# One addition and one reciprocal for both groups of heads of a tile, in the first batch of a pooled attention with a feed-forward network

## The chip, the cores and the metric

The kernel runs on one core of one Trainium2 chip. The metric is the device time of one execution in microseconds (us). The engines are TensorE (PE, with PEld for its weight loads), VectorE (DVE), ScalarE (ACT), GpSimd (POOL) and SyncE (SP, which here issues nearly all DMAs).

## What is computed

Attention over pooled keys and values, and then a feed-forward network on its output, all in float32. There are 8 batches of 8 heads with 576 queries of 64 numbers; keys and values are averaged over 8 neighbours, so each query sees 72 keys.

```python
k_p = k.reshape(B, H, Sp, pool, D).mean(axis=3)          # Sp = 72
v_p = v.reshape(B, H, Sp, pool, D).mean(axis=3)
scores = scale * np.matmul(q, k_p.transpose(0, 1, 3, 2))
scores = scores - np.max(scores, axis=-1, keepdims=True)
attn = np.exp(scores)
attn = attn / (np.sum(attn, axis=-1, keepdims=True) + 1e-09)
...
x = attn_out.transpose(0, 2, 1, 3).reshape(B * S, H * D)  # 4608 x 512
h = x @ w_in                                              # 512 x 2048
g = np.maximum(0.01 * h, h)
return g @ w_out                                          # 2048 x 512
```

## The kernel before

**The whole.** The network's two products take nearly all of TensorE's time. Each factor is split into a high and a low part and a product is three matmuls (lines 905 to 907 for the first layer, 931 to 933 for the second). The weights are split on the chip too: `convert` (lines 201 to 212) turns a raw block of `w_in` or `w_out` into its two parts with two ACT steps, three DVE steps, one more ACT step (line 211) and one more DVE step (line 212). The intermediate `w_t` lies in PSUM in this part of the program.

**The first batch.** Nothing of the network can start before the first 512 rows of `x` are there, so batch 0 is done by itself ahead of it, from 0 to about 46 us, while the first blocks of weights are converted beside it (`c` in the list below). Its 576 queries are five tiles `t` of 128 rows (the last has 64), in three pieces `j`: tiles 0 and 1, tiles 2 and 3, tile 4. A tile's eight heads are two groups `g` of four. The steps are:

- `q{t}`: transposes the queries of a tile on TensorE (`pq`, line 514) and copies them to `qT`.
- `sa{t}{g}` (`s_unit`): the scores of one group on TensorE (`pss`, line 542), minus the row maximum by DVE (line 550), the exponentials by ACT, one instruction a head, with the row sums read out after each (line 552). Maximum and sum lie in a tile `red`.
- `sb{t}{g}` (`norm_unit`): DVE adds 1e-9 to the four sums (line 563) and takes their reciprocals (line 564), POOL multiplies the exponentials with them into `at`, in two instructions (lines 566 and 570).
- `pu{t}{g}`: transposes `at` on TensorE (`pp`, line 634) and splits it into a high part by ACT (636) and a low part by DVE (639 and 643).
- `au{j}{g}`: multiplies with the pooled values (`pa`, lines 658 to 661) and splits the result into `xh` (ACT, 675) and `xl` (DVE, 676).
- `vu`: places the pooled values: `pvm` on TensorE (448), `v_hi` by ACT (456), `v_lo` by DVE (459), `v_parts` (480, 481), `pv` (486) and `v_rem` (489).

**What sets the order.** The list FIRST writes the steps out. TensorE executes in exactly the order of the list (its schedule is manual). For ACT, DVE, POOL and SP a scheduler with a cost model of its own chooses the order from the dependencies and the place in the list; each engine then works strictly in that order, so an instruction that waits holds up all that stand behind it on its engine. The PSUM tiles of batch 0 go round six banks (`bank`): a TensorE step can start when the step six before it has been read out. So `pp` of tile 1, group 1, takes the bank of `pvm`, which `v_lo` is the last to read; `pss` of tile 4 takes the banks of the last two `pa`, which `xl` reads last.

Batch 1 uses `norm_unit` as well, group by group, and later batches `norm_via`; both take the 1e-9 from the tile `tiny`.

Of the kernel before, what the change touches and what calls it, by code (L numbers as in the profile page):

```python
# [10 lines left out]
F32 = mybir.dt.float32  # L11
# [4 lines left out]
ALU = mybir.AluOpType  # L16
# [8 lines left out]
def tile_pooled_attention_ffn(  # L25
# [9 lines left out]
    nc = tc.nc  # L35

    P = 128
# [24 lines left out]
        WHOLE, WHOLE, WHOLE,  # L62
    ]
    FIRST = (
# [3 lines left out]
    )  # L68
# [6 lines left out]
    const = ctx.enter_context(tc.tile_pool(name="const", bufs=1))  # L75
    wts = ctx.enter_context(tc.tile_pool(name="wts", bufs=1))
    one = ctx.enter_context(tc.tile_pool(name="one", bufs=1))
    two = ctx.enter_context(tc.tile_pool(name="two", bufs=2))
# [3 lines left out]
    four = ctx.enter_context(tc.tile_pool(name="four", bufs=4))  # L82
# [6 lines left out]
    make_identity(nc, ident)  # L89


    marks = const.tile([P, 5], F32, name="marks")
    copies = marks[:, 0:4]
    nc.vector.tensor_reduce(
        out=copies, in_=ident.rearrange("p (h c j) -> p c h j", h=4, c=4), axis=AX.XY, op=ALU.add
# [42 lines left out]
        "lo": const.tile([P, 2, PMAX], F32R, name="pT_lo"),  # L138
    }

    tiny = const.tile([P, 4], F32, name="tiny")
    nc.gpsimd.memset(tiny, 1e-9)

    warm = const.tile([P, 1], F32, name="warm")
# [79 lines left out]
    def bank(b, name):  # L224
        nonlocal turn
        pool, tag = banks[turn % len(banks)] if b == 0 else banks[0]
        turn += 1
        return pool.tile([P, NK, P], F32, tag=tag, name=name)
# [271 lines left out]
    def q_unit(b, t, qr):  # L500
# [17 lines left out]
        else:  # L518
# [3 lines left out]

    WIDE = {("at", 1): (8, 0), ("at", 2): (8, 1), ("at", 3): (7, 0),
            ("e", 1): (7, 1), ("e", 2): (6, 0), ("e", 3): (6, 1)}
    wides = {}

    def wide_at(b, t, nm):
        return b == 0 and (nm, t) in WIDE

    def wide(b, t, g, nm, shape):  # L530
        if (nm, t) not in wides:
            wides[nm, t] = spare(*WIDE[nm, t], [P, 2, *shape], F32, f"{nm}{b}_{t}")
        return wides[nm, t][:, g]

    def s_unit(b, t, g, qT):

        n = tiles[b][t][1]
        pss = bank(b, f"pss{b}_{t}_{g}")
        sc = pss.rearrange("a p x -> a (p x)")[:, : 4 * SP]
        for i in range(2):  # L540
            p = 2 * g + i
            nc.tensor.matmul(  # L542
                sc[:, 2 * SP * i : 2 * SP * (i + 1)], qT[:, p, :],
                kT[:, p, :, :].rearrange("d i s -> d (i s)"), start=True, stop=True,
            )
        scv = sc.rearrange("a (h s) -> a h s", s=SP)
        e = wide(b, t, g, "e", [4, SP]) if wide_at(b, t, "e") else two.tile([P, 4, SP], F32, tag="e", name=f"e{b}_{t}_{g}")
        red = four.tile([P, 2, 4], F32, tag="red", name=f"red{b}_{t}_{g}")
        mx, sm = red[:, 0, :], red[:, 1, :]
        nc.vector.tensor_reduce(out=mx[:n], in_=scv[:n], axis=AX.X, op=ALU.max, negate=True)  # L550
        for h in range(4):
            ins = nc.scalar.activation(  # L552
                e[:n, h, :], scv[:n, h, :], AF.Exp, bias=mx[:n, h : h + 1],
                accum_out=sm[:n, h : h + 1],
            )
        if b == 0:
            anchor["act"] = ins
        return e, sm

    def norm_unit(b, t, g, e, sm):  # L560
        n = tiles[b][t][1]
        eng = nc.vector if b == 0 and t in NORM_DVE else nc.gpsimd
        nc.vector.tensor_tensor(sm[:n], sm[:n], tiny[:n], op=ALU.add)
        nc.vector.reciprocal(sm[:n], sm[:n])
        at = wide(b, t, g, "at", [3, P]) if wide_at(b, t, "at") else three.tile([P, 3, P], F32, tag="at", name=f"at{b}_{t}_{g}")
        eng.tensor_tensor(
            at[:n, 0:2, :].rearrange("a i (h s) -> a (i h) s", h=2), e[:n, :, 0:MAIN],
            sm[:n].unsqueeze(2).broadcast_to([n, 4, MAIN]), op=ALU.mult,
        )
        ins = eng.tensor_tensor(  # L570
            at[:n, 2, :].rearrange("a (h c s) -> a h c s", h=4, c=4),
            e[:n, :, MAIN:].unsqueeze(2).broadcast_to([n, 4, 4, REM]),
            sm[:n].unsqueeze(2).unsqueeze(3).broadcast_to([n, 4, 4, REM]), op=ALU.mult,
        )
        if b == 0:
            anchor[eng] = ins
        return at

    def norm_via(b, t, g, e, sm):

        n = tiles[b][t][1]
        nc.vector.tensor_tensor(sm[:n], sm[:n], tiny[:n], op=ALU.add)
        nc.vector.reciprocal(sm[:n], sm[:n])  # L583
        at = three.tile([P, 4, 3, 32], F32, tag="at", name=f"at{b}_{t}_{g}")
        for i in range(2):
            nc.gpsimd.tensor_tensor(  # L586
                at[:n, :, i, :].rearrange("a (h f) j -> a h f j", h=2),
                e[:n, 2 * i : 2 * i + 2, 0:MAIN].rearrange("a h (f j) -> a h f j", f=2),
                sm[:n, 2 * i : 2 * i + 2].unsqueeze(2).unsqueeze(3).broadcast_to([n, 2, 2, 32]),
                op=ALU.mult,  # L590
            )
        nc.gpsimd.tensor_tensor(
            at[:n, :, 2, :].rearrange("a h (c s) -> a h c s", c=4),
            e[:n, :, MAIN:].unsqueeze(2).broadcast_to([n, 4, 4, REM]),
            sm[:n].unsqueeze(2).unsqueeze(3).broadcast_to([n, 4, 4, REM]), op=ALU.mult,
        )
        rows = dram.tile([4, n, 96], F32, name=f"rows{b}_{t}_{g}")
        nc.sync.dma_start(
            rows.rearrange("x a y -> a x y"), at[:n].rearrange("a x i j -> a x (i j)")
        )  # L600
        return rows
# [103 lines left out]
    def attention(b):  # L705
# [39 lines left out]
        def sa(t, g):  # L745
            def f():
                st["e", t, g] = s_unit(b, t, g, st["qT", t])
            return f
# [288 lines left out]
    for b in range(2, B):  # L1037
        for j, piece in enumerate(PIECES[b]):
            c = 2 + (2 * TAIL + S * (b - 2) + piece[0][0]) // CH
# [104 lines left out]
```

## Time and profile before

| what | value |
|---|---|
| median of three runs (lowest, highest) | 924.27 us (922.94 to 924.28) |
| the profiled execution: time | 923.48 us |
| the profiled execution: span from first to last instruction | 921.7 us |
| TensorE busy | 895.0 us, 97% of the span |
| VectorE busy | 449.1 us, 49% |
| ScalarE busy | 406.8 us, 44% |
| GpSimd busy | 195.2 us, 21% |
| mean granted TensorE clock | 0.991 of 2.4 GHz |

The profiled execution's time holds its span and 1.8 us around it; it is 0.8 us under the median of the three runs. The share of busy time is a mean over two very different parts: the first batch, in which TensorE waits often, and the network, in which it hardly does. A row of the timeline says when a group of instructions starts (us from the span's start), how long it takes, engine, line, operation, output and inputs, and in brackets how long the engine had been idle and what ended that.

### The profile page before, as it was taken

What the parts mean: (1) busy time and instruction counts of PE and PEld (TensorE: products, weight loads), DVE (VectorE), ACT (ScalarE), POOL (GpSimd) and SP (SyncE); (2) the same over time, 40 slices, a digit from 0 to 9 for tenths busy, and PEclk for the clock granted to TensorE, in tenths of its full rate; (3) what the DMA queues carried; (4) which work ended last, traced back from release to release, by engine and by line L of the source; (5) the groups of instructions that cost most, each with busy time, mean ns of one, the idle gap of its engine ahead of it and who ended that gap; (6) DMA issues with size and microseconds to landing.
All of it is one profiled execution on the core that took longest, in us unless ns stands there. A gap on an engine that the chain in (4) does not pass through costs nothing.

```text
span 921.7 us, 12752 instructions
## 1 busy us (share of the span) xinstructions
PE 895.0 (97%) x4298; PEld 752.9 (82%) x4298; DVE 449.1 (49%) x1088; ACT 406.8 (44%) x1284; POOL 195.2 (21%) x376
## 2 busy tenths in 40 slices
PE   5699999999999999999999999999999999999998
PEld 4578898888888888888888888888888888888886
DVE  6999469545364354444345444544455322412111
ACT  5788569344344434443443344434434333322221
POOL 4511110443434320502132222311121011000000
PEclk9789999999999999999999999999999999999999
DMA  9965231426344422523242423530331011001001
GB/s 266 318 194 171 55 80 49 97 70 176 118 126 117 95 66 75 130 53 87 75 100 66 109 49 97 118 86 1 103 95 43 1 63 44 26 1 46 0 1 46
DMA packets 134833, 81.05 MB, mean 88 GB/s; under 512 B 98544, under 2 KB 119024, under 8 KB 134768
## 3 DMA queue, kind: packets, MB, share of 16 engines
q1 hardware_dynamic: 134624, 80.11, 32.7%
q8 instruction: 34, 0.56, 0.3%
q14 instruction: 31, 0.25, 0.1%
q10 hardware_dynamic: 144, 0.13, 0.0%
HBM read 59.11 MB, written 21.10 MB: 87 GB/s over the span
## 4 chain that ended last, share of the span: by engine, by line
PE 88%; DVE 4%; DMA 3%; ACT 2%; SPq 1%; POOL 1%; issue 1%; POOLq 0%; ACTq 0%
PE ph L905 13%; PE ph L906 13%; PE ph L907 13%; PE acc L931 13%; PE acc L932 13%; PE acc L933 13%; PE pss L542 4%; ACT e L552 1%; PE pa L659 1%; PE pa L661 1%; PE pa L658 1%; PE pa L660 1%; DMA blocks<-rows 1%; DMA k1raw<-in_k_dram 1%; DMA vremraw<-in_v_dram 1%
## 5 line engine op out<-in xcount | busy, mean ns | idle before, releaser
L905 PE MATMUL ph<-xh,w 128*128 128x512 f32 (+1 forms) x608 | 234.1, 385 | 0.8 <-DVE gl L914 0.8
L906 PE MATMUL ph<-xl,w 128*128 128x512 f32 (+1 forms) x608 | 231.2, 380 | 0.3 <-DVE xl L676 0.3
L907 PE MATMUL ph<-xh,w 128*128 128x512 f32 (+1 forms) x608 | 231.1, 380 | 0.0
L931 PE MATMUL acc<-w,gh 128*128 128x512 f32 x576 | 227.2, 394 | 0.0
L932 PE MATMUL acc<-w,gh 128*128 128x512 f32 x576 | 224.5, 390 | 0.0
L933 PE MATMUL acc<-w,gl 128*128 128x512 f32 x576 | 224.5, 390 | 0.0
L914 DVE TENSOR_TENSOR gl<-ph,gh 128x512 fp32r<-128x512 f32 (+1 forms) x152 | 99.7, 657 | 220.9 <-ACT gh L913 216.7
L910 ACT ACTIVATE ph<-ph 128x512 f32<-128x512 f32 (+1 forms) x152 | 85.5, 563 | 255.9 <-PE ph L907 255.2
L905 PEld LDWEIGHTS ph<-xh,w 128*128 128x128 f32 x608 | 115.1, 189 | 21.9 <-DVE gl L914 1.2
L907 PEld LDWEIGHTS ph<-xh,w 128*128 128x128 f32 x608 | 114.9, 189 | 21.6
L906 PEld LDWEIGHTS ph<-xl,w 128*128 128x128 f32 x608 | 115.0, 189 | 21.0 <-DVE xl L676 0.7
L933 PEld LDWEIGHTS acc<-w,gl 128*128 128x128 f32 x576 | 108.1, 188 | 22.8
L931 PEld LDWEIGHTS acc<-w,gh 128*128 128x128 f32 x576 | 108.3, 188 | 21.1
L932 PEld LDWEIGHTS acc<-w,gh 128*128 128x128 f32 x576 | 108.2, 188 | 20.8
L552 ACT ACTIVATE e<-pss,red 128x72 f32<-128x72 f32 (+1 forms) x320 | 97.6, 328 | 54.4 <-DVE red L550 53.0
L586 POOL TENSOR_TENSOR at<-e,red 128x128 f32<-128x128 f32 (+1 forms) x120 | 46.4, 407 | 216.0 <-DVE red L583 127.6
L913 ACT CAST gh<-ph 128x512 fp32r<-128x512 f32 (+1 forms) x152 | 85.8, 565 | 4.1
L552 ACT ACTIVATION_READ_ACCUMULATOR e<-pss,red 128x1 f32 (+1 forms) x320 | 68.4, 214 | 0.0
L614 DVE STREAM_TRANSPOSE pp<-blocks 128x384 f32<-128x384 f32 (+1 forms) x60 | 44.2, 759 | 49.0 <-DMA blocks<-rows 48.6
L550 DVE TENSOR_REDUCE red<-pss 128x4 f32<-128x288 f32 (+1 forms) x80 | 36.0, 453 | 55.4 <-PE pss L542 51.6
L636 ACT CAST pT_hi<-pp 128x384 fp32r<-128x384 f32 (+1 forms) x80 | 36.2, 478 | 56.5 <-DVE pp L614 51.7
L542 PEld LDWEIGHTS pss<-kT,qT 128*128 128x128 f32 x320 | 47.2, 200 | 6.8 <-ACT qT L519 2.0
(129 smaller groups left out, 826.4 us busy)
## 6 DMA issues: line engine op xcount, KB each, us to landing
rows<-at SPq DMA_DIRECT2D x48, 192.0 KB
blocks<-rows SPq DMA_DIRECT2D x48, 192.0 KB
out_dram<-o SPq DMA_DIRECT2D x34, 256.0 KB
w_bits<-in_moe_w_in_dram SPq DMA_DIRECT2D x16, 512.0 KB
w_bits<-in_moe_w_out_dram SPq DMA_DIRECT2D x16, 512.0 KB
q<-in_q_dram SPq DMA_DIRECT2D x96, 64.0 KB
k0raw<-in_k_dram SPq DMA_DIRECT2D x12, 256.0 KB
k1raw<-in_k_dram SPq DMA_DIRECT2D x12, 256.0 KB
```

The source lines that it names most:

```text
L542: nc.tensor.matmul(sc[:, 2 * SP * i : 2 * SP * (i + 1)], qT[:, p, :], kT[:, p, :, :].rearrange("d i s -> d (i s)"), start=True, stop=True,)
L552: ins = nc.scalar.activation(e[:n, h, :], scv[:n, h, :], AF.Exp, bias=mx[:n, h : h + 1], accum_out=sm[:n, h : h + 1],)
L586: nc.gpsimd.tensor_tensor(at[:n, :, i, :].rearrange("a (h f) j -> a h f j", h=2), e[:n, 2 * i : 2 * i + 2, 0:MAIN].rearrange("a h (f j) -> ...
L905: nc.tensor.matmul(ph, w[:, 0, ks], xh[kk][:, r], start=kk == 0, stop=False)
L906: nc.tensor.matmul(ph, w[:, 0, ks], xl[kk][:, r], start=False, stop=False)
L907: nc.tensor.matmul(ph, w[:, 1, ks], xh[kk][:, r], start=False, stop=kk == NK - 1)
L910: nc.scalar.activation(ph, ph, AF.Prelu, alpha=0.01)
L913: casts.append(nc.scalar.copy(gh, ph))
L914: nc.vector.tensor_tensor(gl, ph, gh.bitcast(F32), op=ALU.subtract)
L931: nc.tensor.matmul(a, gh[:, r], hi, start=first, stop=False)
L932: nc.tensor.matmul(a, gh[:, r], lo, start=False, stop=False)
L933: nc.tensor.matmul(a, gl[:, r], hi, start=False, stop=last)
```

## The change

It touches batch 0 alone, apart from where the 1e-9 lies. The maxima and sums of both groups of a tile go into one tile `reds[t]`; the step `sb{t}0` adds 1e-9 to all eight sums in one instruction and takes their reciprocals in one, and `sb{t}1` only multiplies. In FIRST both groups' scores of tiles 0 and 1 now stand in front of the first normalisation. The constant is one column of `marks`, read with a stride of zero.

```diff
     FIRST = (
-        "lk ku q0 q1 sa00 sb00 sa01 sb01 lv sa10 sb10 sa11 sb11 q2 sa20 sa21 vu pu00 pu10 c c q3 "
+        "lk ku q0 q1 sa00 sa01 sb00 sb01 lv sa10 sa11 sb10 sb11 q2 sa20 sa21 vu pu00 pu10 c c q3 "
...
-    marks = const.tile([P, 5], F32, name="marks")
+    marks = const.tile([P, 6], F32, name="marks")
...
-    tiny = const.tile([P, 4], F32, name="tiny")
+    tiny = marks[:, 5:6]
...
-        red = four.tile([P, 2, 4], F32, tag="red", name=f"red{b}_{t}_{g}")
+        if b == 0:
+            if g == 0:
+                reds[t] = two.tile([P, 2, 2, 4], F32, tag="reds", name=f"red{b}_{t}")
+            red = reds[t][:, :, g, :]
+        else:
+            red = four.tile([P, 2, 4], F32, tag="red", name=f"red{b}_{t}_{g}")
...
-        nc.vector.tensor_tensor(sm[:n], sm[:n], tiny[:n], op=ALU.add)
-        nc.vector.reciprocal(sm[:n], sm[:n])
+
+        both = reds[t][:n, 1].rearrange("a g h -> a (g h)") if b == 0 else sm[:n]
+        if b or g == 0:
+            nc.vector.tensor_tensor(both, both, tiny[:n].broadcast_to(both.shape), op=ALU.add)
+            nc.vector.reciprocal(both, both)
...
-        nc.vector.tensor_tensor(sm[:n], sm[:n], tiny[:n], op=ALU.add)
+        nc.vector.tensor_tensor(sm[:n], sm[:n], tiny[:n].broadcast_to([n, 4]), op=ALU.add)
```

The order on TensorE stays as it was in every instruction. On the other engines the scheduler makes another order. Eight added lines shift the numbers: lines 550, 552, 563, 564 and 566 of before are lines 555, 557, 571, 572 and 574 of the change.

**VectorE, tiles 1 and 2**, before. In `red_1_1`, the first number is the tile, the second the group, and a third one is a buffer's:

```order
L550 TENSOR_REDUCE red_2_0_290<-pss_2_0_286 128x4
L563 TENSOR_TENSOR red_1_1_269<-red_1_1_269,tiny 128x4
L550 TENSOR_REDUCE red_2_1_299<-pss_2_1_296 128x4
L564 RECIPROCAL red_1_1_269<-red_1_1_269 128x4
L481 SCALAR_TENSOR_TENSOR v_parts<-vremsum_131,v_parts 32x64 x2
L489 TENSOR_TENSOR v_rem<-pv_318,heads 128x512
L563 TENSOR_TENSOR red_2_0_290<-red_2_0_290,tiny 128x4
L564 RECIPROCAL red_2_0_290<-red_2_0_290 128x4
L517 COPY qT_3_354<-pq_3_349 128x512
L563 TENSOR_TENSOR red_2_1_299<-red_2_1_299,tiny 128x4
L564 RECIPROCAL red_2_1_299<-red_2_1_299 128x4
L459 SCALAR_TENSOR_TENSOR v_lo<-pvm_305,v_hi 64x4x64 x2
```

And in the change (`red_1_251` is the one tile of both groups of tile 1):

```order
L572 RECIPROCAL red_0_217<-red_0_217 128x8
L571 TENSOR_TENSOR red_1_251<-red_1_251,marks 128x8
L572 RECIPROCAL red_1_251<-red_1_251 128x8
L481 SCALAR_TENSOR_TENSOR v_parts<-vremsum_130,v_parts 32x64 x2
L555 TENSOR_REDUCE red_2_283<-pss_2_0_279 128x4
L555 TENSOR_REDUCE red_2_283<-pss_2_1_289 128x4
L489 TENSOR_TENSOR v_rem<-pv_310,heads 128x512
L459 SCALAR_TENSOR_TENSOR v_lo<-pvm_297,v_hi 64x4x64 x2
L517 COPY qT_3_346<-pq_3_341 128x512
L571 TENSOR_TENSOR red_2_283<-red_2_283,marks 128x8
L572 RECIPROCAL red_2_283<-red_2_283 128x8
L647 TENSOR_TENSOR pT_lo<-pp_0_0_313,pT_hi 128x2x128
```

The maxima of tile 2 now stand behind tile 1's addition, which needs both groups' sums, and behind `v_parts`; `v_lo` stands ahead of `qT_3` and of tile 2's addition.

**ScalarE at the same place**, before:

```order
L480 ACTIVATE v_parts<-vremsum_131 32x64 x2
L552 ACTIVATE e_2_289,red_2_0_290<-pss_2_0_286,red_2_0_290 128x72 x4
L552 ACTIVATE e_2_289,red_2_1_299<-pss_2_1_296,red_2_1_299 128x72 x4
L456 ACTIVATE v_hi<-pvm_305 64x4x64 x2
L636 CAST pT_hi<-pp_0_0_321 128x3x128
```

And in the change:

```order
L480 ACTIVATE v_parts<-vremsum_130 32x64 x2
L456 ACTIVATE v_hi<-pvm_297 64x4x64 x2
L557 ACTIVATE e_2_282,red_2_283<-pss_2_0_279,red_2_283 128x72 x4
L557 ACTIVATE e_2_282,red_2_283<-pss_2_1_289,red_2_283 128x72 x4
L644 CAST pT_hi<-pp_0_0_313 128x3x128
```

`v_hi` has moved from behind tile 2's exponentials to ahead of them.

**VectorE, tile 3**, before (`w_t` and `w` are blocks of weights in conversion):

```order
L563 TENSOR_TENSOR red_3_0_411<-red_3_0_411,tiny 128x4
L639 TENSOR_TENSOR pT_lo_1_1_461<-pp_2_1_462,pT_hi_1_1_460 128x2x128
L643 SCALAR_TENSOR_TENSOR pT_hi_1_1_460<-pp_2_1_462,marks,pT_hi_1_1_460 128x128
L564 RECIPROCAL red_3_0_411<-red_3_0_411 128x4
L212 TENSOR_TENSOR w_0_342<-w_t_343,w_0_342 128x512
L203 TENSOR_SCALAR w_t_479<-w_bits_160 128x512
L563 TENSOR_TENSOR red_3_1_420<-red_3_1_420,tiny 128x4
L204 SCALAR_TENSOR_TENSOR w_t_479<-w_bits_160,w_t_479 128x512
L564 RECIPROCAL red_3_1_420<-red_3_1_420 128x4
L203 TENSOR_SCALAR w_t_427<-w_bits_158 128x512
L207 ISA w_t_479<-w_bits_160,w_t_479 128x1024
L639 TENSOR_TENSOR pT_lo<-pp_3_0_487,pT_hi 128x2x128
```

And in the change:

```order
L212 TENSOR_TENSOR w_0_334<-w_t_335,w_0_334 128x512
L203 TENSOR_SCALAR w_t_466<-w_bits_159 128x512
L571 TENSOR_TENSOR red_3_401<-red_3_401,marks 128x8
L204 SCALAR_TENSOR_TENSOR w_t_466<-w_bits_159,w_t_466 128x512
L572 RECIPROCAL red_3_401<-red_3_401 128x8
L203 TENSOR_SCALAR w_t_416<-w_bits_157 128x512
L207 ISA w_t_466<-w_bits_159,w_t_466 128x1024
L204 SCALAR_TENSOR_TENSOR w_t_416<-w_bits_157,w_t_416 128x512
L207 ISA w_t_416<-w_bits_157,w_t_416 128x1024
L212 TENSOR_TENSOR w_1_465<-w_t_466,w_1_465 128x512
L647 TENSOR_TENSOR pT_lo<-pp_3_0_474,pT_hi 128x2x128
L651 SCALAR_TENSOR_TENSOR pT_hi<-pp_3_0_474,marks,pT_hi 128x128
```

Group 0 of tile 3 no longer has an addition and a reciprocal of its own ahead of the conversions, and three more conversion steps (204, 207 and 212) stand between the reciprocal and `pT_lo` of tile 3, group 0.

## Rows read from the trace of the kernel before

**Rows 1.** Busy time of each engine in four stretches: the stretch, its length, then busy us (and instructions) of PE, PEld, DVE, ACT and POOL, the granted TensorE clock as a share of 2.4 GHz, the DMA share and GB/s.

```profile
24.00:36.00 12.00, 6.33 (x33) 5.53 (x32) 11.97 (x30) 9.14 (x32) 9.61 (x12) 0.81 1.11 324
36.00:48.00 12.00, 9.15 (x37) 7.63 (x37) 11.86 (x28) 8.55 (x28) 2.47 (x5) 0.64 0.96 323
48.00:60.00 12.00, 10.93 (x49) 7.97 (x49) 10.74 (x27) 12.00 (x29) 2.58 (x4) 0.84 0.57 176
54.00:60.00 6.00, 6.00 (x27) 4.56 (x27) 5.43 (x14) 6.00 (x13) 0.00 (x0) 0.72 0.68 225
```

**Rows 2.** TensorE alone after the first batch: busy us (and instructions), granted clock, DMA share, GB/s.

```profile
62.00:921.00 859.00, 853.54 (x4100) 1.00 0.29 75
```

**Rows 3.** What TensorE waited for in the whole run: us in total, times, longest.

```profile
PE pp L634 <- POOL at L566: 7.9, 3, 5.2
PE pss L542 <- DVE xl L676: 1.9, 2, 1.1
PE pa L659 <- DVE pT_lo L639: 1.1, 2, 0.8
```

**Rows 4.** Groups of VectorE's instructions from 0 to 60 us, shapes apart: busy us, mean ns, idle before. The first four are the additions and reciprocals of batch 0; the last is a 64-element addition.

```profile
L563 DVE TENSOR_TENSOR red<-red,tiny 128x4 f32<-128x4 f32 x8 | 2.6, 328 | 0.1
L564 DVE RECIPROCAL red<-red 128x4 f32<-128x4 f32 x8 | 1.3, 167 | 0.1
L563 DVE TENSOR_TENSOR red<-red,tiny 64x4 f32<-64x4 f32 x2 | 0.4, 205 | 0.5 <-ACT e L552 0.5
L564 DVE RECIPROCAL red<-red 64x4 f32<-64x4 f32 x2 | 0.3, 170 | 0.1
L264 DVE TENSOR_TENSOR vremsum<-vremraw 64x64 f32<-64x64 f32 x1 | 0.2, 234 | 0.0
```

**Rows 5.** The timeline from 15 to 25 us, tiles 0 to 2 (a selection). The accumulator row at 17.66 is the last sum of tile 1, the exponential at 18.29 the first of tile 2 and the accumulator row at 20.59 its last.

```profile
15.97 0.61 POOL L566 TENSOR_TENSOR at<-e,red 128x256 f32<-128x256 f32 x1 [2.82 <-DVE red L563]
17.66 0.29 ACT L552 ACTIVATION_READ_ACCUMULATOR e<-pss,red 128x1 f32 x1
17.83 0.61 POOL L566 TENSOR_TENSOR at<-e,red 128x256 f32<-128x256 f32 x1
17.98 0.47 DVE L563 TENSOR_TENSOR red<-red,tiny 128x4 f32<-128x4 f32 x1
18.09 0.61 PE L448 MATMUL pvm<-v1raw,addup 128*128 128x128 f32 x4
18.29 0.32 ACT L552 ACTIVATE e<-pss,red 128x72 f32<-128x72 f32 x1
18.38 0.44 DVE L550 TENSOR_REDUCE red<-pss 128x4 f32<-128x288 f32 x1
18.94 0.80 DVE L481 SCALAR_TENSOR_TENSOR v_parts<-vremsum,v_parts 32x64 fp32r<-32x64 f32 x2
20.59 0.24 ACT L552 ACTIVATION_READ_ACCUMULATOR e<-pss,red 128x1 f32 x1
20.68 0.77 ACT L456 ACTIVATE v_hi<-pvm 64x256 fp32r<-64x256 f32 x2
22.46 0.83 DVE L459 SCALAR_TENSOR_TENSOR v_lo<-pvm,v_hi 64x256 fp32r<-64x256 f32 x2
23.43 0.52 PE L634 MATMUL pp<-ident,at 128*128 128x128 f32 x3 [1.80 <-POOL at L566]
23.71 0.36 PE L658 MATMUL pa<-pT_hi,v_hi 128*128 128x256 f32 x1
```

**Rows 6.** The timeline from 28 to 39 us, tile 3 (a selection). The accumulator row at 34.45 is the last sum of tile 3; the two `pp` are its groups 0 and 1, the two `at` on POOL as well.

```profile
28.07 0.41 DVE L676 TENSOR_TENSOR xl<-pa,xh 128x256 fp32r<-128x256 f32 x1
31.98 1.28 POOL L257 TENSOR_TENSOR v1raw<-v1raw 128x512 f32<-128x512 f32 x1
32.51 0.78 DVE L563 TENSOR_TENSOR red<-red,tiny 128x4 f32<-128x4 f32 x1
34.45 0.28 ACT L552 ACTIVATION_READ_ACCUMULATOR e<-pss,red 128x1 f32 x1
35.25 0.90 PE L634 MATMUL pp<-ident,at 128*128 128x128 f32 x3 [5.18 <-POOL at L566]
36.10 0.16 DVE L564 RECIPROCAL red<-red 128x4 f32<-128x4 f32 x1
36.77 0.67 DVE L207 CUSTOM_DVE_ANT_0 w_t<-w_bits,w_t 128x1024 uint16<-128x1024 uint16 x1
37.07 0.90 PE L634 MATMUL pp<-ident,at 128*128 128x128 f32 x3 [0.92 <-POOL at L566]
38.67 0.58 PE L661 MATMUL pa<-pT_hi,v_rem 128*128 128x256 f32 x1
```

**Rows 7.** The timeline from 41 to 54 us, tile 4 and the network's first matmuls (a selection): `pss` of tile 4, the network's first matmul, `at` of group 0, `pp` of group 0 and the first matmul that waits for its low part.

```profile
43.47 0.73 PE L542 MATMUL pss<-kT,qT 128*128 128x144 f32 x4 [1.14 <-DVE xl L676]
45.79 0.80 PE L905 MATMUL ph<-xh,w 128*128 128x512 f32 x1
48.41 0.61 POOL L566 TENSOR_TENSOR at<-e,red 64x256 f32<-64x256 f32 x1 [7.37 <-DVE red L564]
50.00 0.40 PE L634 MATMUL pp<-ident,at 64*128 64x64 f32 x3
53.36 0.30 PE L659 MATMUL pa<-pT_lo,v_hi 128*128 128x64 f32 x1 [0.83 <-DVE pT_lo L639]
```

More of the change, by code (lines that the diff above doesn't have):

```diff
@@ L524, in tile_pooled_attention_ffn @@
             ("e", 1): (7, 1), ("e", 2): (6, 0), ("e", 3): (6, 1)}
-    wides = {}
+    wides, reds = {}, {}
     def wide_at(b, t, nm):
```

## The prediction

> **What bounds the kernel now.** I first read the busy time by stretch. From 62 us on TensorE is busy for 853.5 of 859 us [rows 2]: whatever the first batch and the first blocks of weights gain or lose ahead of that is gained or lost at the end, nearly one for one. Nothing that the change touches lies behind it, except additions that read their constant with another stride. So the question is only when TensorE's first 62 us are over. In them VectorE sets the pace: it is busy for 11.97 and 11.86 of 12 us from 24 to 48 us, with TensorE at 6.33 and 9.15 [rows 1]. TensorE's waits say through what: for POOL's `at` (three waits, 7.9 us, one of them 5.2), for `xl` and for `pT_lo` of VectorE [rows 3]. From 48 to 60 us ScalarE is full as well, 12.00 of 12 [rows 1]. The granted clock is 0.81, 0.64 and 0.84 in these three stretches [rows 1], and TensorE had waited ahead of each fall.
>
> **What is removed.** Five additions and five reciprocals. By mean durations, four of 328 ns and one of 205, four of 167 and one of 170 [rows 4], that is 1.31 + 0.20 + 0.67 + 0.17 = 2.35 us of VectorE. Those that stay are eight numbers wide instead of four. No row has that width; below, it costs nothing, above, it costs what 64 numbers cost, 234 ns against 167 [rows 4], and as 60 more numbers make 67 ns, four make 4. I take nothing for it, nor for the stride of zero, and no DMA is added. So 2.35 us is the ceiling of the gain.
>
> **What is added** is a wait: the joint addition needs the sums of both groups. I follow it through the three places where VectorE's order changes, with the durations of the rows and each engine in its new order.
>
> **Tiles 0 to 2.** Tile 0's first `at` started at 15.97; it now waits for one more group of exponentials, which take (20.83 - 18.29) / 2 = 1.3 us [rows 5], and VectorE fills that with its other work. Nobody waits: TensorE takes tile 1's last `at` only when `v_lo` has freed its bank. Tile 1's joint addition can start when its last sum is there, 17.95, and that is when the last separate one started, 17.98 [rows 5]. The difference is what stands behind it. Before, the first maximum of tile 2 had been taken ahead of it. Now addition 0.47, reciprocal 0.16 and `v_parts` 0.80 come first, to 19.4, and then two maxima of 0.44 less overlap, to 20.2. Tile 2's first exponential starts at 19.9 instead of 18.29 and its last sum comes at 22.4 instead of 20.83 [rows 5]. ScalarE uses the gap: `pvm` ends at 18.70, so `v_hi` (0.77) is done at 19.5 and not at 21.45. It reaches the first `pT_hi` at 22.4 instead of 21.5, 0.9 late, and the weights' steps behind it are as late. On VectorE `v_lo` comes at 20.9 to 21.7 instead of 22.46 to 23.29, and the `pp` that started at 23.43 goes at 22.7. (The row names POOL for that wait, but tile 1's `at` was long there; it was `v_lo`, which ends 0.14 us ahead of it.) So `pa` starts at 23.2 instead of 23.71 [rows 5], 0.5 early. But VectorE then has to wait for the weights' ScalarE steps. Between 0.5 early and 0.9 late I take **0.3 late** at the first `xl`, 28.07 before [rows 6], nearer the middle, since VectorE can do one weight step and the `pT` of two tiles while it waits.
>
> One price in this is a stall. The addition at 17.98 takes 0.47 and the one at 32.51 takes 0.78, and they end, at 18.45 and 33.29, when a POOL instruction on SBUF ends, at 18.44 and 33.26 [rows 5, 6]. The Trainium skill, SBUF — State Buffer, section "SBUF: two separate sides", says why: a VectorE operation with two SBUF inputs and a GpSimd operation exclude each other for the whole instruction. By that rule, which speaks against the joint addition of tile 1 as much as against the separate one, since it meets tile 0's second multiplication, the trace agrees. In numbers of the rows: stretched to 0.47 the sum is as above; if it ran in the reciprocal's 0.16 everything behind it would come 0.3 earlier, and the sum below would be 0.45 and not 0.75.
>
> **Tile 3.** Here the saving shows. From the first `xl` to the last reciprocal VectorE needed 36.26 - 28.07 = 8.2 us; without group 0's addition (0.78) and reciprocal (0.16) it needs 7.3 [rows 6], and from 28.4 it would end at 35.7, if the sums are there. They are at 34.73 [rows 6], and the joint addition comes up at about 34.7. So the reciprocal ends 0.5 earlier than group 1's did, but POOL now begins group 0 only then: group 0's `pp`, 35.25 before, goes at about 36.4, and group 1's, 37.07 before, one POOL group later, at about 37.4 (two multiplications of up to 0.61 [rows 5] to a group). TensorE needs both before `pa` of the second piece, so **the last `pp` is 0.3 late** although VectorE was early. Then three more weight steps stand ahead of `pT_lo`. The first conversion step 207 ends at about 36.9, three steps of 0.6 each (0.67 in the row, less the overlap) make 38.7, `pT_lo` and `pT_hi` 39.3: the matmul that needs them (line 661), 38.67 before [rows 6], goes at about 39.3, **0.6 late**.
>
> **Tile 4.** `pa`, and `xl` behind it, carry this on, with VectorE doing two weight steps (1.2 us) early that stood behind the last `xl` before. `pss` of tile 4 waits for an `xl`; I put it at 44.7 instead of 43.47 and the network's first matmul at 46.5 instead of 45.79 [rows 7]. The joint addition waits for both groups, so `at` starts at about 50.1 instead of 48.41 and its `pp` goes at 50.8 instead of 50.00. VectorE meanwhile stands idle, then needs its five weight steps, and the matmul that waits for `pT_lo`, 53.36 before [rows 7], goes at 54.1: **0.75 late**. From there TensorE works through.
>
> **The sum** is the last of these delays, since each holds the ones ahead of it: +0.75 us. On the profiled execution's own time that is 923.48 + 0.75 = 924.2 us. That execution is 0.8 us below the median of the runs shown, so in terms of the median it is 924.27 + 0.75 = **925.0 us**. Each of the three places can be off by some 0.5 us (a step of the weights more or less); together -0.1 to +1.6, so 924.2 to 925.9.
>
> **Rivals.**
>
> *The count of instructions decides (faster).* VectorE is full from 24 to 48 us, and it has 2.35 us less to do. If the joint additions find their sums there, because ScalarE runs ahead, the whole saving reaches 62 us: 924.27 - 2.35 = 921.9. For it: tile 3, where VectorE comes half a microsecond earlier. Against it: tiles 1 and 4, where it would wait. The Trainium skill has a rule for this, VectorE: DVE Perf Modes, section "Rules for kernel authors": in a chain of VectorE operations the count of operations is what to make small. The trace agrees that four numbers cost nearly what 64 cost, and by the rule alone the change would be faster.
>
> *A further stretch at the lower clock (slower).* From 54 to 60 us TensorE is busy all the time at a granted clock of 0.72 [rows 1]; this is part of the time at 1.2 GHz, and costs 6 x 0.28 = 1.7 us on work that is on the path. Ahead of it TensorE had waited for `pT_hi` and `pT_lo` of tile 4. If the later `at` of tile 4 makes TensorE stop ahead of `pp` as well, at 50 us, the same may come once more there: 925.0 + 1.7 = 926.7. It decides from the point where TensorE is through with the first block before `at` is there; in my sum the two come within 0.3 us of each other.
>
> *One such stretch less.* If TensorE's pauses at 52 us close instead, the 1.7 us come back: 925.0 - 1.7 = 923.3.
>
> That the change does nothing is excluded: the orders on VectorE and ScalarE show it.
>
> **How the numbers follow.** Forecast 0.50; count of instructions 0.24; further stretch 0.17; one stretch less 0.09. A measurement of this kernel can tell about 0.2% from no change, 1.85 us. The forecast's range lies within that; of the faster rival 0.20 lies beyond (its waits can leave part of the 2.35), of the last 0.01. So faster 0.21, slower 0.17, the same 0.62. The range takes the ceiling of the gain and the further stretch: 921.8 to 926.8.
>
> **What would show it.** Right: the first exponential of tile 2 at 19.9; `v_lo` ending at 21.7; the first `pa` at 23.2; `pp` of tile 3 in close sequence at 36.4 and 37.4; `at` of tile 4 at 50.1; the first `pT_lo` matmul of tile 4 at 54.1. Wrong: TensorE reaching that matmul ahead of 53.0 (the saving has passed through), or a granted clock from 48 to 60 us well off 0.84.

## The result, and the profile after

The changed kernel takes 935.37 us (934.81 to 935.85, 4 runs) against 924.1 us for the kernel before (922.94 to 924.28, 4 runs): a ratio of 1.013, 95% interval 1.0118 to 1.0142, **slower by 11 us**. The prediction, 925.0 with a range of 921.8 to 926.8, was wrong. The profiled execution of the changed kernel took 935.85 us, its span 934.1, at a mean granted clock of 0.993.

I looked for the 12.4 us between the spans (934.1 - 921.7) in the first batch, since the change is there. They are not there. Busy time by stretch, with the columns of [rows 1]:

```profile
24.00:36.00 12.00, 4.31 (x29) 3.61 (x29) 11.54 (x29) 9.96 (x33) 9.98 (x14) 0.88 1.10 327
36.00:48.00 12.00, 9.01 (x38) 7.30 (x39) 11.71 (x26) 7.93 (x21) 3.26 (x7) 0.64 0.93 304
48.00:60.00 12.00, 10.40 (x49) 7.73 (x47) 10.14 (x25) 12.00 (x34) 2.71 (x4) 0.91 0.53 165
54.00:60.00 6.00, 5.14 (x30) 4.08 (x30) 6.00 (x17) 6.00 (x13) 0.00 (x0) 1.00 0.67 187
```

TensorE got through 30 matmuls from 54 to 60 us, against 27 before, and at full clock instead of 0.72 [rows 1]; from 48 to 60 us the clock was 0.91 instead of 0.84. A landmark behind the first batch is ScalarE's cast of `gh` for the fifth block of the network; the timeline of the kernel before has it at 78.18, that of the changed one at 78.42:

```profile
78.18 0.59 ACT L913 CAST gh<-ph 128x512 fp32r<-128x512 f32 x1
```

```profile
78.42 0.59 ACT L921 CAST gh<-ph 128x512 fp32r<-128x512 f32 x1
```

So **0.24 us are lost by 78 us, and the other 12.2 behind it**, where TensorE's instructions and their order are the same. TensorE is busy there and at full clock (the columns are those of [rows 2]; it was x4100 before):

```profile
62.00:921.00 859.00, 856.61 (x4063) 1.00 0.29 74
```

It gets through 37 fewer matmuls in the same 859 us, 4,063 instead of 4,100. The matmuls themselves are slower. The costliest groups of the page (busy us, mean ns of one, idle before), the kernel before first:

```profile
L905 PE MATMUL ph<-xh,w 128*128 128x512 f32 (+1 forms) x608 | 234.1, 385 | 0.8 <-DVE gl L914 0.8
L906 PE MATMUL ph<-xl,w 128*128 128x512 f32 (+1 forms) x608 | 231.2, 380 | 0.3 <-DVE xl L676 0.3
L907 PE MATMUL ph<-xh,w 128*128 128x512 f32 (+1 forms) x608 | 231.1, 380 | 0.0
L931 PE MATMUL acc<-w,gh 128*128 128x512 f32 x576 | 227.2, 394 | 0.0
L932 PE MATMUL acc<-w,gh 128*128 128x512 f32 x576 | 224.5, 390 | 0.0
L933 PE MATMUL acc<-w,gl 128*128 128x512 f32 x576 | 224.5, 390 | 0.0
```

and the changed one:

```profile
L913 PE MATMUL ph<-xh,w 128*128 128x512 f32 (+1 forms) x608 | 235.6, 388 | 0.8 <-DVE gl L922 0.8
L915 PE MATMUL ph<-xh,w 128*128 128x512 f32 (+1 forms) x608 | 232.8, 383 | 0.0
L914 PE MATMUL ph<-xl,w 128*128 128x512 f32 (+1 forms) x608 | 230.8, 380 | 0.2 <-DVE xl L684 0.2
L939 PE MATMUL acc<-w,gh 128*128 128x512 f32 x576 | 230.7, 400 | 0.0
L940 PE MATMUL acc<-w,gh 128*128 128x512 f32 x576 | 227.6, 395 | 0.0
L941 PE MATMUL acc<-w,gl 128*128 128x512 f32 x576 | 227.1, 394 | 0.0
```

In the order of the lines the means rise by 3, 0 and 3 ns in the first layer and by 6, 5 and 4 in the second: 608 x 6 + 576 x 15 ns = 12.3 us, the whole loss. Two things in these rows are easily misread. Busy time rises because each matmul takes longer, so "busier" is here the symptom and no good sign. And the idle time before them is as small as before, so no wait explains it.

It is no other engine either. From 880 to 900 us the DMA engines rest, GpSimd does nothing, VectorE is busy for 2.08 of 20 us in either kernel and ScalarE for less than before, and matmuls are lost all the same, 88 instead of 90 (the columns of [rows 1], the kernel before first):

```profile
880.00:900.00 20.00, 20.00 (x90) 16.58 (x89) 2.08 (x3) 4.51 (x8) 0.00 (x0) 1.00 0.00 0
880.00:900.00 20.00, 20.00 (x88) 16.31 (x87) 2.08 (x3) 3.68 (x7) 0.00 (x0) 1.00 0.00 1
```

In the timeline of the kernel before, 24 matmuls start between these two `acc` rows at 884.48 and 889.92, 226.7 ns apart on average (5.44 us / 24):

```profile
884.48 0.39 PE L931 MATMUL acc<-w,gh 128*128 128x512 f32 x1
884.71 0.39 PE L932 MATMUL acc<-w,gh 128*128 128x512 f32 x1
884.94 0.39 PE L933 MATMUL acc<-w,gl 128*128 128x512 f32 x1
...
889.92 0.39 PE L931 MATMUL acc<-w,gh 128*128 128x512 f32 x1
```

In the changed kernel the same 24 take 5.56 us, 231.7 ns each:

```profile
884.36 0.40 PE L939 MATMUL acc<-w,gh 128*128 128x512 f32 x1
884.60 0.41 PE L940 MATMUL acc<-w,gh 128*128 128x512 f32 x1
884.84 0.40 PE L941 MATMUL acc<-w,gl 128*128 128x512 f32 x1
...
889.92 0.40 PE L939 MATMUL acc<-w,gh 128*128 128x512 f32 x1
```

What differs there is where the operands lie in SBUF, the memory of these tiles (a matmul reads two operands there, a moving one, named first in the rows, and a stationary one). In this program tiles take slots of 32 bytes in a partition. The change drops `tiny` (16 bytes, one slot) from the pool `const`, so that everything behind it moves down by 32 bytes, and adds `reds` to the pool `two`: two buffers of 64 bytes, so that everything behind that pool, `gh` and `gl` among it, moves up by 128. The starts of the network's operands, worked out from the tile sizes, modulo 256 bytes: `w` 64, `xh` and `xl` 64, `gh` and `gl` 64 before; 32, 32 and 160 after. The slices that a matmul takes of them lie whole multiples of 512 bytes behind these starts, so they have the same remainders. A matmul of the second layer now reads two operands whose starts are 128 bytes apart modulo 256.

### The profile page after: what moved, and what is told of

The parts are those of the page before. It is cut to its first block, busy times and chain, and to the rows that moved or that the text cites. A ratio compares the mean times of both kernels' runs of the same rounds, so it can differ in the third digit from the quotient of the medians.

```text
span 934.1 us, 12737 instructions
## 1 busy us (share of the span) xinstructions
PE 904.4 (97%) x4298; PEld 751.0 (80%) x4298; DVE 448.3 (48%) x1078; ACT 407.0 (44%) x1284; POOL 195.2 (21%) x376
## 4 chain that ended last, share of the span: by engine, by line
PE 86%; DMA 4%; DVE 4%; ACT 3%; SPq 2%; POOL 1%; issue 1%; DVEq 0%; POOLq 0%; ACTq 0%
PE acc L939 13%; PE acc L940 13%; PE acc L941 13%; PE ph L913 13%; PE ph L915 13%; PE ph L914 13%; PE pss L542 4%; DMA blocks<-rows 2%; ACT e L557 1%; PE pa L666 1%; PE pa L667 1%; PE pa L669 1%; PE pa L668 1%; DMA v1raw<-in_v_dram 1%; SPq L310 1%
## 5 line engine op out<-in xcount | busy, mean ns | idle before, releaser
L915 PE MATMUL ph<-xh,w 128*128 128x512 f32 (+1 forms) x608 | 232.8, 383 | 0.0
L914 PE MATMUL ph<-xl,w 128*128 128x512 f32 (+1 forms) x608 | 230.8, 380 | 0.2 <-DVE xl L684 0.2
L939 PE MATMUL acc<-w,gh 128*128 128x512 f32 x576 | 230.7, 400 | 0.0
L940 PE MATMUL acc<-w,gh 128*128 128x512 f32 x576 | 227.6, 395 | 0.0
L941 PE MATMUL acc<-w,gl 128*128 128x512 f32 x576 | 227.1, 394 | 0.0
L922 DVE TENSOR_TENSOR gl<-ph,gh 128x512 fp32r<-128x512 f32 (+1 forms) x152 | 99.9, 658 | 228.0 <-ACT gh L921 227.2
L644 ACT CAST pT_hi<-pp 128x384 fp32r<-128x384 f32 (+1 forms) x80 | 36.4, 482 | 56.0 <-DVE pp L622 50.8
L542 PEld LDWEIGHTS pss<-kT,qT 128*128 128x128 f32 x320 | 45.2, 192 | 6.8 <-issue 1.8
```

What stands on the lines that cost most here:

```text
L542: nc.tensor.matmul(sc[:, 2 * SP * i : 2 * SP * (i + 1)], qT[:, p, :], kT[:, p, :, :].rearrange("d i s -> d (i s)"), start=True, stop=True,)
L914: nc.tensor.matmul(ph, w[:, 0, ks], xl[kk][:, r], start=False, stop=False)
L915: nc.tensor.matmul(ph, w[:, 1, ks], xh[kk][:, r], start=False, stop=kk == NK - 1)
L922: nc.vector.tensor_tensor(gl, ph, gh.bitcast(F32), op=ALU.subtract)
L939: nc.tensor.matmul(a, gh[:, r], hi, start=first, stop=False)
L940: nc.tensor.matmul(a, gh[:, r], lo, start=False, stop=False)
```

## The experiments

A hole is a pool of one unused tile; it moves all pools behind it and no instruction: the order on every engine stays. The edits are shown against the kernel before, or against the changed one where the name begins with after. The table has all kernels with their starts modulo 256, the median, the ratio to the runs of the kernel before on the same chip (923.04 us for the four from after_even to g_shifted, 923.35 for the four from after_128 to x_alone, 922.54 for the last four), and the mean distance in ns from the start of a 512-wide matmul of the network to that of TensorE's next matmul, from the starts in the traces between 160 and 905 us (distances over 262 ns, with something in between, left out), for the three lines of the first layer and the three of the second.

| kernel | `w`, `x`, `gh` | us | ratio (95%) | first layer | second layer |
|---|---|---|---|---|---|
| before | 64, 64, 64 | 924.1 | | 227.0 / 227.3 / 227.3 | 226.9 / 227.2 / 227.2 |
| changed | 32, 32, 160 | 935.37 | 1.013 (1.0118 to 1.0142) | 231.1 / 227.1 / 230.5 | 233.9 / 232.9 / 231.8 |
| after_even | 64, 64, 192 | 934.87 | 1.0127 (1.011 to 1.0144) | 230.7 / 227.1 / 230.2 | 233.9 / 232.7 / 231.7 |
| all_shifted | 96, 96, 96 | 922.74 | 0.9995 (0.9985 to 1.0004) | 226.8 / 227.1 / 227.3 | 226.7 / 226.8 / 227.3 |
| x_shifted | 64, 96, 128 | 939.24 | 1.0172 (1.0157 to 1.0187) | 232.8 / 232.8 / 233.3 | 232.8 / 233.3 / 233.1 |
| g_shifted | 64, 64, 96 | 932.8 | 1.0106 (1.0089 to 1.0124) | 228.2 / 227.5 / 229.6 | 232.2 / 232.7 / 233.5 |
| after_128 | 32, 32, 32 | 923.86 | 1.0001 (0.9992 to 1.001) | 227.3 / 227.0 / 227.4 | 227.0 / 227.0 / 227.4 |
| before_128 | 64, 64, 192 | 934.12 | 1.0114 (1.01 to 1.0127) | 230.8 / 227.2 / 230.1 | 233.8 / 232.8 / 231.7 |
| before_256 | 64, 64, 64 | 923.37 | 0.9997 (0.9987 to 1.0006) | 226.9 / 227.4 / 227.3 | 226.8 / 227.3 / 227.2 |
| x_alone | 64, 96, 64 | 934.39 | 1.0118 (1.0104 to 1.0131) | 234.3 / 232.3 / 233.7 | 232.8 / 227.7 / 229.2 |
| const_256 | 64, 64, 64 | 923.57 | 1.0007 (0.9999 to 1.0016) | 227.8 / 227.5 / 227.2 | 227.7 / 227.2 / 227.2 |
| after_const_256 | 64, 64, 64 | 923.9 | 1.0012 (1.0003 to 1.0021) | 227.7 / 227.4 / 227.4 | 227.5 / 227.1 / 227.5 |
| order_alone | 64, 64, 64 | 922.48 | 1.0 (0.9991 to 1.0009) | 227.0 / 227.3 / 227.4 | 226.8 / 227.2 / 227.3 |
| joint_2_to_4 | 32, 32, 32 | 922.31 | 0.9994 (0.9984 to 1.0003) | 227.2 / 226.9 / 227.6 | 226.9 / 227.0 / 227.4 |

Theory A was that starts off the multiples of 64 bytes are slow (A1 of the moving operand, A2 of the stationary one), theory B that something else in the change slows TensorE: the new order, the wider steps or the constant's column. Theory C came after the first four runs: the distance between the two operands of a matmul decides.

**after_even.** The changed kernel, all starts back at multiples of 64:

```diff
+    pad0 = ctx.enter_context(tc.tile_pool(name="pad0", bufs=1))
+    pad0.tile([P, 8], F32, name="hole0")
     wts = ctx.enter_context(tc.tile_pool(name="wts", bufs=1))
```

> The changed kernel with a hole of 32 bytes ahead of the pool of the weights, so that weights, x, gh and gl begin at multiples of 64 bytes again, as in the kernel before (in the change they begin 32 bytes off, since the tile tiny is gone); the order of every engine is that of the change. Theory A (where the operands of the network's matmuls begin sets their rate): about 924.9 us, the 0.75 us of the first batch alone, matmul starts 227 ns apart. Theory B (the new order, the wider steps or the constant's column slow TensorE): it stays at 935 us, with starts 230 to 234 ns apart.

Measured 934.87 us: as slow as the change, so theory A falls; theory B had it so.

**all_shifted.** The same hole in the kernel before: all operands move by 32 bytes together.

> The kernel before with a hole of 32 bytes ahead of the pool of the weights, so that all operands of the network's matmuls begin 32 bytes off a multiple of 64; nothing of the change is in it and the order of every engine is that of before. Theory A: about 935 us (924 + 11), the first batch's timeline as before. Theory B: 924 us.

922.74 us and 227 ns. A common shift costs nothing. Theory B expected that too; the next two runs decide against it.

**x_shifted** and **g_shifted.** The kernel before, with holes of 32 bytes: in the first `x` lies 32 off `w` and `gh` 64 off; in the second only `gh` and `gl` lie 32 off.

```diff
+    pad0.tile([P, 8], F32, name="hole0")      # x_shifted
     one = ctx.enter_context(tc.tile_pool(name="one", bufs=1))
+    pad1.tile([P, 8], F32, name="hole1")      # x_shifted
     two = ctx.enter_context(tc.tile_pool(name="two", bufs=2))
...
+    pad0.tile([P, 8], F32, name="hole0")      # g_shifted
     three = ctx.enter_context(tc.tile_pool(name="three", bufs=3))
+    pad1.tile([P, 8], F32, name="hole1")      # g_shifted
     four = ctx.enter_context(tc.tile_pool(name="four", bufs=4))
```

> The kernel before with x alone (the moving operand of the first layer's matmuls, and queries and sums that share its pool) 32 bytes off a multiple of 64. In the change the first layer's three lines are 4.1, 0 and 3.2 ns slower, 608 of each, 4.4 us at most. A1 (the moving operand's start counts): about 928 us. A2 (the stationary operand's start counts): 924 us. Theory B: 924 us.

> The kernel before with gh and gl alone (the stationary operands of the second layer's matmuls, and at and blocks, which share their pool) 32 bytes off. In the change the second layer's three lines are 7.0, 5.7 and 4.5 ns slower, 576 of each, 9.9 us at most. A1 (moving): 924 us. A2 (stationary): about 932 to 934 us. Theory B: 924 us.

Both are slow, 939.24 and 932.8 us, without any of the change's instructions, so theory B falls. For x_shifted no theory had expected more than 928 us; g_shifted came as A2 had it, but A had fallen with after_even. What the slow kernels have in common is a distance between the two operands. Where both layers have one, all six lines run at 233 ns; where only the second has one, its lines run at 232 to 233.5 and two of the first at 228 and 230.

**after_128, before_128, before_256.** One hole ahead of `three`, of 128 or 256 bytes:

```diff
+    pad0.tile([P, 32], F32, name="hole0")     # [P, 64] in before_256
     three = ctx.enter_context(tc.tile_pool(name="three", bufs=3))
```

> The changed kernel with one hole of 128 bytes ahead of the pool of gh and gl. The start of the multiples of 64 has fallen as a theory; now theory C: what counts is the distance, modulo 256 bytes, between the starts of a matmul's two operands. In the change the pool two is 128 bytes longer (the tile reds), so gh and gl lie 128 bytes off w; with the hole they lie 256 off the distance of before. C: matmul starts 227 ns apart again and 923.0 + 0.75 = 923.8 us, what the first batch alone costs (between 922.5 and 925 by the two sides of that estimate). Theory B (the change's orders or wider steps): 935 us.

> The kernel before with the same hole of 128 bytes ahead of the pool of gh and gl, so that they lie 128 bytes off w as in the change; nothing of the change is in it. C: 934 us, second layer's starts 232 to 234 ns apart and the first layer's 231, 227 and 230 as in the change. B: 923 us.

> The kernel before with a hole of 256 bytes at the same place. C with 256 bytes: 923 us, as before. If the period is 512 bytes or more, or any move of gh and gl counts: 930 us or more.

This is the decisive pair: the same 128 bytes take the loss away from the changed kernel (923.86, ratio 1.0001) and put it into the kernel before (934.12, with the pattern of the changed kernel line by line). 256 bytes do nothing, so the distance counts modulo 256, as far as these distances show. The second layer's groups of after_128 on its page are back at the means of before:

```profile
L941 PE MATMUL acc<-w,gh 128*128 128x512 f32 x576 | 227.3, 395 | 0.0
L943 PE MATMUL acc<-w,gl 128*128 128x512 f32 x576 | 224.5, 390 | 0.0
L942 PE MATMUL acc<-w,gh 128*128 128x512 f32 x576 | 224.4, 390 | 0.0
```

**x_alone.** Holes of 32 bytes ahead of `one` and 224 ahead of `two`: only `x` has a distance.

```diff
+    pad0.tile([P, 8], F32, name="hole0")
     one = ctx.enter_context(tc.tile_pool(name="one", bufs=1))
+    pad1.tile([P, 56], F32, name="hole1")
     two = ctx.enter_context(tc.tile_pool(name="two", bufs=2))
```

> The kernel before with x 32 bytes off w and everything behind it 256 off, so that the first layer's operands are 32 bytes apart modulo 256 and the second layer's 0. C: the first layer's starts about 233 ns apart, the second layer's 227, some 5.6 ns x 3 x 490 = 8.2 us more than before, 931 us; if a slow matmul also hands its delay to the next ones, the second layer is above 227 as well and the time is up to 935 us. A distance that counted for the second layer alone: 923 us.

934.39 us, the counterpart of g_shifted, and near the 935 expected if a slow matmul hands its delay on. The page's groups show which lines pay:

```profile
L909 PE MATMUL ph<-xh,w 128*128 128x512 f32 (+1 forms) x608 | 237.1, 390 | 0.4 <-DVE gl L918 0.4
L911 PE MATMUL ph<-xh,w 128*128 128x512 f32 (+1 forms) x608 | 233.4, 384 | 0.0
L910 PE MATMUL ph<-xl,w 128*128 128x512 f32 (+1 forms) x608 | 233.1, 383 | 0.0
L935 PE MATMUL acc<-w,gh 128*128 128x512 f32 x576 | 229.9, 399 | 0.0
L937 PE MATMUL acc<-w,gl 128*128 128x512 f32 x576 | 225.5, 391 | 0.0
L936 PE MATMUL acc<-w,gh 128*128 128x512 f32 x576 | 224.6, 390 | 0.0
```

The first layer pays throughout; of the second, whose own operands agree, line 935 still pays 5 ns. That a layer without a distance is slowed in part shows here, in g_shifted and in the changed kernel; how the one carries over to the other is not settled.

**const_256** and **after_const_256.** `kT` and `qT`, the operands of the scores, start 128 bytes apart modulo 256 in the kernel before (192 and 64). Holes bring them to one place as well:

```diff
+    pad0.tile([P, 32], F32, name="hole0")
     const = ctx.enter_context(tc.tile_pool(name="const", bufs=1))
+    pad1.tile([P, 32], F32, name="hole1")     # [P, 40] in after_const_256
     wts = ctx.enter_context(tc.tile_pool(name="wts", bufs=1))
...
+    pad2.tile([P, 32], F32, name="hole2")     # after_const_256 alone
     three = ctx.enter_context(tc.tile_pool(name="three", bufs=3))
```

> The kernel before with one hole of 128 bytes ahead of the pool `const` and one of 128 bytes ahead of the pool `wts`: the weights and all pools behind them move by 256 bytes (their distances to each other stay), the tiles of `const` (kT, v_hi, v_lo among them) by 128, so that kT and qT, whose starts were 128 bytes apart modulo 256, now agree. Theory C (a matmul whose two operands start at different places modulo 256 bytes is slow) expects the scores' matmuls to get faster where they follow each other closely, the network's steps to stay at 227 ns, and in all 0 to 4 us less than before: 919 to 923.5. That only the network's wide matmuls are touched: 923.0, no difference that can be measured.

> The changed kernel with holes of 128 bytes ahead of `const`, 160 ahead of `wts` and 128 ahead of `three`: weights, `x`, `gh` and `gl` and kT all start at the same place modulo 256. Theory C expects it within 0.1% of const_256, since the change's first batch is worth nothing in the end (after_128 923.86 against 923.35 for before): 919 to 924. That the change of the first batch is worth something by itself which the rate of the matmuls hides would show as a difference of over 1 us between this kernel and const_256.

No gain: 923.57, ratio 1.0007. The scores' matmuls (120 to 900 us) took 285 ns before and 286 in const_256:

```profile
L542 PE MATMUL pss<-kT,qT 128*128 128x144 f32 x240 | 34.2, 285 | 0.0
```

```profile
L546 PE MATMUL pss<-kT,qT 128*128 128x144 f32 x240 | 34.3, 286 | 0.0
```

So this part of my expectation missed: the rule is shown for the network's 512-wide matmuls, and the 144-wide ones of the scores do not follow it. They differ from the network's in their type as well (plain float32, where the network's operands are float32r, `fp32r` in the rows), so whether the width or the type matters isn't shown. The changed kernel with the same starts takes 923.9, within 0.04% of const_256: what the change does to the first batch is too small for these timings of whole executions.

**order_alone** and **joint_2_to_4** halve the change. The first has only the new list FIRST. The second is the changed kernel with the old list, and joint additions in tiles 2 to 4 alone, with a hole of 128 bytes ahead of `three`:

```diff
-        if b == 0:
+        if b == 0 and t > 1:
...
-        if b or g == 0:
+        if b or t < 2 or g == 0:
```

> The kernel before with only the new list FIRST (both groups' scores of tiles 0 and 1 ahead of the normalisations); additions and reciprocals stay one per group, and no address moves. If the order of tiles 0 to 2 is what delays tile 4 and takes away the stretch at the lower clock, this kernel shows the granted clock from 54 to 60 us near 1.00 and the first matmul with tile 4's low part near 54.5; if it is the joint addition of tiles 3 and 4, both stay as before (0.72, 53.4). In time 922 to 925 either way, steps of 227 ns.

> The counterpart: the old list FIRST, one addition and reciprocal for both groups in tiles 2, 3 and 4 alone, and 128 bytes more ahead of `three` so that all starts agree modulo 256. If the wait for both groups' sums in tiles 3 and 4 makes the delay, `at` of tile 4 starts near 50 us instead of 48.41, the first matmul with tile 4's low part goes near 54.5 instead of 53.36, and the granted clock from 54 to 60 us is near 1.00; if not, all three stay near before. In time 922 to 925 either way, steps of 227 ns.

In both the steps are 227 ns and the time is that of before (ratios 1.0 and 0.9994). In joint_2_to_4 `at` of tile 4 started at 49.94, as expected, and the first matmul with tile 4's low part went at 54.05, against 53.36 [rows 7]: the wait for both groups in tiles 2 to 4 makes about half of the delay, 0.7 of the change's 1.3 us. In order_alone it went at 53.49, and the profiles of kernels with the old order have it anywhere from 53.11 to 53.53. But the clock from 54 to 60 us did not follow it, as I had expected it to: it was 1.00 in both, in order_alone with hardly a delay.

The eight profiles of kernels with the old order and nothing but holes say why: it changes from execution to execution, with the same order of instructions. (Between executions of the kernel before itself, of 921 to 926 us each, the mean clock goes from 0.989 to 0.994; 6 us at 0.72 are worth 0.002 of that.) In four (before, const_256, before_128, all_shifted) that stretch had 0.72 and the landmark came at 78.18 to 78.36; in the other four (before_256, g_shifted, x_shifted, x_alone) it had 1.00 and the landmark came at 77.21 to 77.34. before_256, whose matmuls have the rate of before:

```profile
54.00:60.00 6.00, 5.57 (x30) 4.36 (x30) 5.88 (x16) 6.00 (x13) 0.00 (x0) 1.00 0.70 224
```

```profile
77.32 0.59 ACT L915 CAST gh<-ph 128x512 fp32r<-128x512 f32 x1
```

So executions with the stretch are 1.0 us later at 78 us, and by chance the profiled execution of before was one. Not all of this need be the stretch's doing: at tile 4's first low part these four are already 0.25 us later (53.44 against 53.19 in the mean). The four profiles with the whole change in the first batch (changed, after_even, after_128, after_const_256) were all without it, with the landmark at 78.24 to 78.45. Like with like, **the change's first batch is about 1 us late**: by the means 1.1 (77.28 and 78.36), order_alone (77.59) 0.3 and joint_2_to_4 (77.83) 0.55. They are alike from 54 to 60 us only; from 48 to 54 us the clock was 0.84 to 1.00 in the four of the old order and 0.75 to 0.96 in the four of the change. before_256 and after_128, which agree there too (0.96), are 0.9 apart (77.32 and 78.24). What decides whether an execution has the stretch, and whether the new order can have it at all, stays open.

## Why the prediction was wrong

**The step that failed** is the first: "Nothing that the change touches lies behind it, except additions that read their constant with another stride", and with it that what happens ahead of 62 us decides. I took the diff's `tiny` and `reds` for what they do and gave their places no price. Those places set the rate of 1,728 matmuls of the second layer, and in part of 1,824 of the first, and cost 12.2 of the 12.4 us between the two profiled executions. In the medians it is 11.5 us (935.37 against 923.86 of after_128) or 10.8 (934.12 of before_128 against 923.35). No rival had this mechanism, and so the range, up to 926.8, held none of it. With the starts brought together (after_128, 923.86 against 923.35, or 1.0001) the time lies within the -0.1 to +1.6 us over before that the sum allowed.

**The first batch** went much as worked out. Rows of the changed kernel's timeline for the steps that the prediction named:

```profile
17.97 0.39 DVE L571 TENSOR_TENSOR red<-red,marks 128x8 f32<-128x8 f32 x1 [1.32 <-ACT v_parts L480]
20.02 0.32 ACT L557 ACTIVATE e<-pss,red 128x72 f32<-128x72 f32 x1 [0.61 <-DVE red L555]
20.93 0.85 DVE L459 SCALAR_TENSOR_TENSOR v_lo<-pvm,v_hi 64x256 fp32r<-64x256 f32 x2
23.35 0.38 PE L666 MATMUL pa<-pT_hi,v_hi 128*128 128x256 f32 x1
28.60 0.75 DVE L684 TENSOR_TENSOR xl<-pa,xh 128x256 fp32r<-128x256 f32 x2
36.53 1.83 PE L642 MATMUL pp<-ident,at 128*128 128x128 f32 x6 [6.52 <-POOL at L574]
39.31 0.58 PE L667 MATMUL pa<-pT_lo,v_hi 128*128 128x256 f32 x1 [0.72 <-DVE pT_lo L647]
45.10 1.59 PE L542 MATMUL pss<-kT,qT 128*128 128x144 f32 x8 [1.60 <-DVE xl L684]
46.44 0.50 PE L913 MATMUL ph<-xh,w 128*128 128x512 f32 x1
50.53 0.61 POOL L574 TENSOR_TENSOR at<-e,red 64x256 f32<-64x256 f32 x1 [9.66 <-ACT w_bits L201]
54.65 0.30 PE L667 MATMUL pa<-pT_lo,v_hi 128*128 128x64 f32 x1 [1.03 <-DVE pT_lo L647]
```

- Tiles 0 to 2: the first exponential of tile 2 at 20.02 (19.9 forecast), `v_lo` to 21.78 (21.7), the first `pa` at 23.35 (23.2): right. The first `xl` came at 28.60, 0.53 us late where I had taken 0.3.
- Tile 3: both `pp` from 36.53 (36.4), the wait for `pT_lo` to 39.31 (39.3): right.
- Tile 4: `pss` at 45.10 (44.7), the network's first matmul at 46.44 (46.5), `at` at 50.53 (50.1), the low part's matmul at 54.65 (54.1). The direction was right and the term too small: +1.29 us against the 53.36 of [rows 7] instead of +0.75, since `at` came 0.4 later than I had put it, behind the later `pss`.
- The landmark at 78 us is only 0.24 later than in the profiled execution of before, because that one had the stretch at the lower clock from 54 to 60 us, and executions that have it are 1.0 later. Against those without it the change is 0.9 to 1.1 us late there: the sum of 0.75 had the right sign and was somewhat too small. I had taken a stretch that four of eight profiles have for a property of the kernel, and so the two rivals on it, 1.7 us each way, were bets on chance. The clock from 48 to 60 us, 0.91 where I had named "well off 0.84" as a sign of being wrong, was for the same reason no good sign. At 1.0 us at most the stretch was also priced too high, since TensorE, at full clock, waits for other engines instead (busy for 5.57 of the 6 us in before_256, for 6.00 before [rows 1]).
- The prices of the instructions: the groups of 0 to 60 us, with the columns of [rows 4], are

```profile
L571 DVE TENSOR_TENSOR red<-red,marks 128x8 f32<-128x8 f32 x4 | 0.9, 218 | 1.4 <-ACT v_parts L480 1.3
L572 DVE RECIPROCAL red<-red 128x8 f32<-128x8 f32 x4 | 0.8, 197 | 0.1
```

With 0.4 us for the 64-row ones, that is 2.1 us instead of 4.6: 2.5 saved, 2.35 forecast. Eight numbers cost the reciprocal 30 ns more than four (197 against 167), where I had taken nothing; the 234 ns that I had held against 167 were those of an addition, not of a reciprocal. The addition at 17.97 again ended when a multiplication on POOL ended (18.36 and 18.34), so the stall stayed, as assumed; at 0.39 us it was shorter.

The waits of TensorE answer to [rows 3]: for `at` fewer, the longest of them longer; for `pT_lo` more and longer; and one for `pT_hi`, 1.4 us ahead of the `pa` from which that first `xl` is made.

```profile
PE pp L642 <- POOL at L574: 6.7, 2, 6.5
PE pa L667 <- DVE pT_lo L647: 2.4, 4, 1.0
PE pss L542 <- DVE xl L684: 1.6, 1, 1.6
PE pa L666 <- DVE pT_hi L651: 1.4, 1, 1.4
```

The faster rival, 2.35 us, did not come: VectorE waits in tile 1 (1.32 us ahead of the addition at 17.97) and in tile 4, as the prediction's argument against it had it.

## What to carry to other kernels

A change that adds or drops a tile, however small, moves every tile behind it: ask of each edit which big operands change their distance modulo 256 bytes, and bring the two operands of a hot matmul to the same start modulo 256 with a hole, if the same matmuls turn out slower. (This is shown for 512-wide float32r matmuls alone.) When a kernel gets slower, first find by a landmark in which part the time was lost, and compare the mean durations of the same instructions there, before reasoning about the part that was edited. Two kernels whose allocations differ are compared fairly only once the big operands lie alike.

## What the runs showed of the hardware

The rate of back-to-back 512-wide matmuls depends on where their two operands start. With equal starts modulo 256 bytes in both layers they follow each other in 227 to 228 ns; 32, 64 or 128 bytes apart in 231.7 to 234.3 (64 only together with 32 in the other layer), and the network's 3,552 matmuls then take 9.8 to 16.2 us longer (g_shifted 932.8 and x_shifted 939.24, against 923.04 us). A common shift of 32 bytes and a distance of 256 cost nothing. It holds with all DMA at rest, and no wait in the profile names it. Matmuls whose own operands agree are slowed too, by up to 6 ns, where those of the other layer have a distance; why is open.

The Trainium skill, SBUF — State Buffer, section "Who interferes with whom", gives TensorE two independent read ports, one for the moving operand and one for weight loads, and says that TensorE never waits on anyone. As far as other engines go these runs don't speak against it; that the two reads are independent of each other they do speak against, by 5 to 7 ns in 227. That the two reads meet in one part of the memory would fit, but is only argued: no run looked at it.
